# First block converted during attention, routing handed out by VectorE time, two groups' routing overlapped: attention and top-2 experts on one core

## Chip, core and metric

One core of a Trainium2 chip runs the whole program in one launch. The metric is device time in microseconds (us); smaller is better. Engines: PE (TensorE, matmul), PEld (its weight loads), DVE (VectorE), ACT (ScalarE), POOL (GpSimd) and SP (SyncE, which here only issues DMAs). Each engine takes its instructions in program order and waits on semaphores for the others.

## What is computed

```python
# attention: 8 batches x 8 heads, 576 positions in 9 chunks of 64, head size 64
scores = q_c @ k_c.T / sqrt(64);  attn = softmax(scores);  x = (attn @ v_c)   # -> x: 4608 tokens x 512
# experts: E = 8, hidden 1024
logits = x @ w_gate
noisy  = logits + log1p(exp(x @ w_noise)) * noise
top2   = argpartition(-noisy, 2)[:, :2];  top2_w = softmax over the two
for e in range(8):
    for k in range(2):
        mask = top2[:, k] == e
        h = maximum(x[mask] @ w1[e], 0)
        out[mask] += top2_w[mask, k] * (h @ w2[e])
```

## The kernel before

**Turns.** The 4608 tokens are 36 tiles of 128. The function `attend(it)` (L676) is one turn; it works on several tiles at different depths: `scores(it)` (L410, PE), the row maximum and subtraction (L418, L423, DVE) and the exponential (L428, ACT) of tile it; the transposes of the probabilities of tile it-1 (L430); the products with v (`pv`, L438) and the division (`norm_a/b/c`, L446 to L455) of tile it-2, which give the tile `xs`; and `x_trans` (L457) of tile it-3, which stores `xs` to a DRAM buffer `xbuf` by an SP DMA and transposes it for the gate. Once per four tiles come `gate_mm` (L468) and `gate_sum` (L476). Loads of q, k and v come in pairs of tiles, five buffers each (L363, L366); `xs` has three buffers.

**Routing.** The tiles form groups of 8, 8, 4, 8 and 8 (L160). `route(g)` (L487) is a Python generator, and its `yield`s only decide where its instructions stand in each engine's program order. Its steps: softplus of the noise logits on ACT (L500 to L503); noisy logits on DVE (L507 to L515); maxima and their indices (L520, L524); one-hots (L529 to L535); the *rank products* on PE (L541, L543), into PSUM bank 6; positions in the lists (L546 to L588, DVE); then for each tile r of the group a *list product*: `gohp` on POOL (L604) and ACT (L605, L606), `geq` on DVE (L608), `grhs` on POOL (L612; DVE for the last group), and two matmuls on PE (`place`, L596), two tiles behind. At the end the sums are added (L630), and `finish_lists` (L203) and `gather` (L233, POOL indirect DMAs) fetch the rows of a block of expert 0: block 0 after group 1, block 1 after group 3, block 2 after group 4.

**Who steps the routing.** `step_route(n)` (L651) advances the first generator of the list by n yields, each worth the same whatever it costs. A turn gives 2 yields between maximum and subtraction and 8 after the division (STEPS, L677; 3 and 12 from turn 33 on). To leave ACT and PE time, the routing has three stretches of 7 empty yields (IDLE, L485). A group's generator starts only when the one before it is done.

**Experts.** Each expert's list is cut into three blocks of 384 tokens or a little more. `x_tile(i, k)` (L277) is the *conversion* of 128 gathered rows of block i: for the first blocks, 4 PE transposes (L286) into PSUM bank 0 or 1, a rounded copy `xh` on ACT (L293) and the rest `xl` on DVE (L294). `layer1` (L305) is, for each of 8 hidden slices f, 4 steps d of 3 matmuls (`three`, L296, L303); its result leaves by `hh` (ACT, L321) and `hl` (DVE, L322); for block 0 it alternates between banks 0 and 1. `layer2` (L344) is 24 matmuls for each 128 tokens and starts in bank 6. While block 0 is in layer 1, the last four turns (`tail`, L733: what is left of tiles 33 to 35) and the splitting of the second weight matrix (`w_split`, L130, L138 on DVE) stand between its matmuls, and `hook_tail` (L737) gives 2 yields to the routing after each d step; `hook2_r` (L775) gives 2 after each f of layer 2, and layer 1 of block 1 gives 1 after each d.

After the 36 turns the kernel runs `attend(NT)`, then the three conversions of block 0 (L729, L730), then `layer1(0)`.

Of the kernel before, what the change touches and what calls it, by code (L numbers as in the profile page):

```python
# [60 lines left out]
def kernel(ctx, tc, qT, kT, vh, wgn, noise, w1, w2, out, caps=CAPS):  # L61
# [102 lines left out]
    xg = ctx.enter_context(tc.tile_pool(name="xg", bufs=5))  # L164

# [17 lines left out]
    XG, XH, HT, BX, BH, OB = {}, {}, {}, {}, {}, {}  # L183
    rot = {"xg": 0, "tr": 0, "l1": 0, "l2": 0}
# [92 lines left out]
    def x_tile(i, k):  # L277
# [5 lines left out]
        if i < NPE:  # L283
            src = bank("tr").rearrange("p (d n) -> p d n", d=ND)[:, :, 0:r]
# [103 lines left out]
    for j in range(3):  # L388
        load_q(j)
        load_k(j)  # L390
        load_v(j)
# [8 lines left out]
    load_q(3)  # L400
    load_k(3)
    load_v(3)
# [20 lines left out]
    def soft_sub(t, mx):  # L423
        PR[t] = work.tile([P, 512], FT, name="pr")
        nc.vector.tensor_tensor(by_head(PR[t]), sco(t), mx[:, :, :, None].to_broadcast([P, 2, 4, 64]), OP.subtract)
# [27 lines left out]
    def norm_c(t):  # L453
        XS[t] = work.tile([P, DM], FT, name="xs", bufs=3)
        nc.vector.tensor_tensor(by_head(XS[t]), pvb[:, :, :, 0:64], RC[t].to_broadcast([P, 2, 4, 64]), OP.mult)  # L455
# [29 lines left out]
    IDLE = 7  # L485

    def route(g):  # L487
# [16 lines left out]
        for _ in range(IDLE):  # L504
            yield

        V.scalar_tensor_tensor(u, u, -1.0, y, op0=OP.add, op1=OP.subtract)  # L507
        yield
        V.tensor_sub(sp, sp, u)
        yield  # L510
        V.scalar_tensor_tensor(sp, z[:, :, 1, :], 0.0, sp, op0=OP.max, op1=OP.add)
        yield
        V.tensor_mul(sp, sp, nz[:, t0:t0 + G, :])
        yield
        V.tensor_add(sp, sp, z[:, :, 0, :])  # L515
        yield
        m = gate.tile(n8, FT, name="gm")
        mi = gate.tile(n8, U32, name="gmi")
        for r in range(G):
            V.max(m[:, r], sp[:, r])  # L520
            if r % 2:
                yield
        for r in range(G):
            V.max_index(mi[:, r], m[:, r], sp[:, r])  # L524
            if r % 2:
                yield
        oh = gate.tile([P, 2, G, NE], FT, name="goh")
        for k in range(2):
            V.tensor_tensor(oh[:, k], be(e_row), br(mi[:, :, k]), OP.is_equal)  # L529
            yield  # L530
# [4 lines left out]
        V.tensor_sub(ex, m[:, :, 1], m[:, :, 0])  # L535
        yield
        nc.scalar.activation(ex, ex, AF.Exp)
        for _ in range(IDLE):
# [5 lines left out]
        for _ in range(IDLE):  # L544
            yield
# [4 lines left out]
        yield  # L550
# [3 lines left out]
        yield  # L554
# [3 lines left out]
        yield  # L558
        if g == LAST:
# [10 lines left out]
            yield  # L570
# [8 lines left out]
            yield  # L579
# [3 lines left out]
        yield  # L583
        pj = gate.tile([P, 2, 2, G], I32, name="gpj")
        pf = gate.tile([P, 2, 2, G], FT, name="gpf")
# [3 lines left out]
        yield  # L589

        lp = PS[:, 7, 0:2 * NL]
# [9 lines left out]
        for r in range(G):  # L601
# [8 lines left out]
            yield  # L610
# [3 lines left out]
            yield  # L614
            yield
            built.append((r, ohp, rhs))
            if len(built) > 2:
                yield
                place(*built.pop(0))
            yield  # L620
        while built:
            for _ in range(3):
                yield
            place(*built.pop(0))
        yield
# [6 lines left out]
        for i in EARLY:  # L632
            if g == EARLY[i]:
                js = slice(blocks[0][i][0][0], blocks[0][i][-1][0] + 1)
                finish_lists(lid0[i], lwt0[i], lfl[:, js, 0], a4[:, :, js, 0])
                gather(i)
        if g == LAST:
            for c in range(2):
                for js in (slice(0, NJ // 2), slice(NJ // 2, NJ)):
# [6 lines left out]
                    yield  # L646
# [15 lines left out]
    def finish_route(until=lambda: not routing):  # L662
        while not until():
            step_route(1)
# [11 lines left out]
    def attend(it):  # L676
        STEPS = 2 if it < 33 else 3  # L677
        if it % 2 == 0 and it >= 2 and it // 2 + 3 < NT // 2:
            load_q(it // 2 + 3)
            load_k(it // 2 + 3)  # L680
# [11 lines left out]
        if it - 5 >= 0 and (it - 5) % 4 == 3:  # L692
            gate_sum((it - 5) // 4)
            if grp_of[it - 5] != grp_of.get(it - 4):
                routing.append(route(grp_of[it - 5]))
        if it - 4 >= 0 and (it - 4) % 4 == 3:
            gate_mm((it - 4) // 4)
        if it < NT:
            mx = soft_max(it)
            step_route(STEPS)  # L700
            soft_sub(it, mx)
            soft_exp(it)
        if 0 <= it - 2 < NT:
            norm_b(it - 2)
            norm_c(it - 2)
            step_route(4 * STEPS)
        if it % 2 == 1 and it >= 3 and (it - 3) // 2 + 4 < NT // 2:
            load_v((it - 3) // 2 + 4)
# [12 lines left out]
    def block_bufs(q):  # L721
        pool = pb.enter_context(tc.tile_pool(name=f"blk{q}", bufs=1))
        HN = BN if q == 0 else 3 * P
        BX[q] = tuple(pool.tile([P, ND, BN], FR, name=f"x{c}{q}") for c in "hl")
# [4 lines left out]
    for k in range(len(blocks[0][0])):  # L729
        x_tile(0, k)  # L730

# [5 lines left out]
    def hook_tail(f, d):  # L737
# [6 lines left out]
        else:  # L744
            step_route(2)

    for i in range(NBL + 1):
# [27 lines left out]
        def hook2_r(k, f):  # L775
            hook2_f(k, f)
            step_route(2)
            if i == 0 and f == 6 and k < len(nxt):
                x_tile(1, k)
            if i == 1 and (k, f) in LATE:  # L780
# [8 lines left out]
        if i < NBL:  # L789
            layer1(i, hook1, hook_tail if i == 0 else lambda f, d: step_route(1))  # L790
# [160 lines left out]
```

## Time and profile before

| What | us |
|---|---|
| runs | 1015.87, 1020.08, 1020.49; median 1020.08 |
| the profiled execution: own time | 1020.72 |
| its span, first to last instruction | 1018.9 (1.8 lie around it) |
| PE busy in the span | 966.8 (95%) |
| first and last row maximum (36 turns) | 5.4 and 147.6 |
| last attention matmul group ahead of the first expert block | 152.69 |
| first layer-1 matmul | 158.73 |
| first layer-2 matmul | 187.10 |

A row of the timeline is: start, duration, engine, source line, operation, written tile and read tiles, count, and in brackets how long the engine had stood idle and what released it. A row of the waits is: the waiting engine and tile, what it waited for, total us, number of waits, longest one.

### The profile page before, as it was taken

To read this page: it belongs to the slowest core of one execution; us is meant where nothing else is said; L and a number is where in the kernel's file an instruction comes from. 1 tells how busy PE (TensorE), PEld (TensorE's weight loads), DVE (VectorE), ACT (ScalarE), POOL (GpSimd) and SP (SyncE) were. 2 spreads that over 40 slices of the span, in tenths; PEclk is the share of its full clock that TensorE was granted. 3 is DMA by queue.
4 is the path that set the end of the run, shared out by engine and by line. 5 is a ranking of instruction groups with operands and counts; after the bars stand their busy time and mean duration, and the time that the engine had idled before them with its cause. 6 is when DMAs were issued, how large, how long until landed. Compare 5 with 4: busy or idle time off the path is not lost.

```text
span 1018.9 us, 18401 instructions
## 1 busy us (share of the span) xinstructions
PE 966.8 (95%) x7353; PEld 862.0 (85%) x7353; DVE 458.5 (45%) x1001; ACT 310.4 (30%) x689; POOL 480.9 (47%) x619
## 2 busy tenths in 40 slices
PE   5888888999999999999999999999999999999994
PEld 4666767897889899989998999899989998899983
DVE  4676774644525353345334533453345334434311
ACT  3575855331314032213221322232223221323100
POOL 1033623324577668346834684477347825611111
PEclk9997988999999999999999999999999999999998
DMA  9999865233341543243423343344343334411212
GB/s 353 363 320 325 293 209 206 75 103 69 88 108 45 110 137 80 44 99 117 102 42 97 112 106 52 94 119 104 57 109 120 73 66 101 136 17 27 32 24 41
DMA packets 52233, 121.53 MB, mean 119 GB/s; under 512 B 8320, under 2 KB 9216, under 8 KB 52144
## 3 DMA queue, kind: packets, MB, share of 16 engines
q1 hardware_dynamic: 31984, 81.64, 22.2%
q0 software_dynamic: 20160, 38.69, 20.6%
q8 instruction: 58, 0.95, 0.4%
q14 instruction: 31, 0.25, 0.1%
HBM read 81.56 MB, written 38.73 MB: 118 GB/s over the span
## 4 chain that ended last, share of the span: by engine, by line
PE 82%; DVE 1%; ACT 1%; issue 0%; POOL 0%; ACTq 0%; DVEq 0%
PE PS L303 79%; PE PS L332 1%; PE PS L596 1%; PE PS L286 0%; DVE xl L294 0%; ACT xh L293 0%; DVE xs L455 0%; POOL gohp L604 0%; DVE o L341 0%; PE PS L220 0%; PE PS L443 0%; PE PS L470 0%; PE PS L482 0%; ACT gohp L605 0%; PE PS L222 0%
## 5 line engine op out<-in xcount | busy, mean ns | idle before, releaser
L258 POOL DMA_INDIRECT xg<-xbuf,piece x257 | 261.2, 1016 | 76.4 <-issue 68.4
L303 PE MATMUL PS<-xh,w1h 128*128 128x384 f32 (+2 forms) x768 | 263.0, 343 | 2.4 <-DVE xl L294 1.4
L303 PE MATMUL PS<-xl,w1h 128*128 128x384 f32 (+2 forms) x768 | 260.6, 339 | 0.3 <-DVE xl L294 0.3
L303 PE MATMUL PS<-xh,w1l 128*128 128x384 f32 (+2 forms) x768 | 260.6, 339 | 0.0
L303 PE MATMUL PS<-w2h,hh 128*128 128x512 f32 x584 | 229.4, 393 | 0.0
L303 PE MATMUL PS<-w2h,hl 128*128 128x512 f32 x584 | 228.2, 391 | 0.0
L303 PE MATMUL PS<-w2l,hh 128*128 128x512 f32 x584 | 228.1, 391 | 0.0
L270 POOL DMA_INDIRECT out<-o,lid x73 | 117.0, 1602 | 235.0 <-DVE o L341 213.5
L322 DVE SCALAR_TENSOR_TENSOR hl<-PS,hh 128x384 fp32r<-128x384 f32 (+1 forms) x192 | 107.1, 558 | 218.8 <-ACT hh L321 187.2
L321 ACT ACTIVATE hh<-PS 128x384 fp32r<-128x384 f32 (+1 forms) x192 | 94.1, 491 | 363.4 <-PE PS L303 314.3
L303 PEld LDWEIGHTS PS<-xh,w1h 128*128 128x128 f32 x768 | 144.4, 188 | 6.2 <-DVE xl L294 1.8
L303 PEld LDWEIGHTS PS<-xl,w1h 128*128 128x128 f32 x768 | 144.5, 188 | 2.3 <-DVE xl L294 0.5
L303 PEld LDWEIGHTS PS<-xh,w1l 128*128 128x128 f32 x768 | 144.4, 188 | 1.0
L341 DVE TENSOR_SCALAR o<-PS,lwt 128x512 f32<-128x512 f32 x73 | 54.5, 748 | 199.1 <-PE PS L303 166.6
L303 PEld LDWEIGHTS PS<-w2h,hl 128*128 128x128 f32 x584 | 109.6, 188 | 23.7
L303 PEld LDWEIGHTS PS<-w2h,hh 128*128 128x128 f32 x584 | 109.6, 188 | 23.3 <-issue 0.8
L303 PEld LDWEIGHTS PS<-w2l,hh 128*128 128x128 f32 x584 | 109.7, 188 | 22.5
L604 POOL TENSOR_SCALAR gohp<-row_p,gpf 128x128 f32<-128x128 f32 x36 | 26.3, 773 | 118.6 <-DVE gpf L588 107.0
L293 ACT ACTIVATE xh<-y 128x512 fp32r<-128x512 f32 x67 | 41.2, 615 | 106.7 <-DVE y L290 84.5
L294 DVE TENSOR_TENSOR xl<-y,xh 128x512 fp32r<-128x512 f32 x67 | 45.1, 673 | 48.3 <-ACT xh L293 31.8
L290 DVE STREAM_TRANSPOSE y<-xg 128x512 f32<-128x512 f32 x67 | 45.6, 680 | 2.4 <-DMA xg<-xbuf,piece 2.4
L138 DVE TENSOR_TENSOR w2l<-st,w2h 128x512 fp32r<-128x512 f32 x64 | 45.1, 705 | 0.0
(139 smaller groups left out, 798.9 us busy)
## 6 DMA issues: line engine op xcount, KB each, us to landing
st<-in_w SPq DMA_DIRECT2D x64, 512.0 KB
out<-zero SPq DMA_DIRECT2D x37, 256.0 KB
vb<-in_vh SPq DMA_DIRECT2D x18, 520.0 KB
xbuf<-xs SPq DMA_DIRECT2D x36, 256.0 KB
qp<-in_qT SPq DMA_DIRECT2D x17, 512.0 KB
kb<-in_kT SPq DMA_DIRECT2D x17, 512.0 KB
xg<-xbuf,piece POOLq DMA_INDIRECT x257
out<-o,lid POOLq DMA_INDIRECT x73
```

Source lines behind the costliest of these rows:

```text
L138: (eng or nc.vector).tensor_sub(lo[:, s], st[:, s], hi[:, s].bitcast(FT))
L258: nc.gpsimd.indirect_dma_start(out=XG[e, j][:, t * P:(t + 1) * P], out_offset=None, in_=xpieces, in_offset=bass.IndirectOffsetOnAxis(ap=pi ...
L270: s = nc.gpsimd.indirect_dma_start(out=to, out_offset=bass.IndirectOffsetOnAxis(ap=rows, axis=0), in_=o, in_offset=None, compute_op=OP.add)
L290: nc.vector.transpose(y[:, 0:4 * r], x[:, 0:4 * r])
L293: nc.scalar.activation(oh, src, AF.Copy)
L294: nc.vector.tensor_sub(ol, src, oh.bitcast(FT))
L303: nc.tensor.matmul(p, a, b, start=first and n == 0, stop=last and n == 2)
L321: nc.scalar.activation(hh[:, 0:m], p, AF.Relu)
L322: nc.vector.scalar_tensor_tensor(hl[:, 0:m], p, 0.0, hh[:, 0:m].bitcast(FT), op0=OP.max, op1=OP.subtract)
L332: nc.tensor.matmul(p[32 * q:32 * q + 32, 0:P], HF[0][:, f, 32 * t:32 * t + 32], w[:, q * P:(q + 1) * P], start=(f == 0), stop=(f == NF - 1))
L341: nc.vector.tensor_scalar(o[0:r], p[0:r], weights_of(i, j)[0:r], None, op0=OP.mult)
L604: nc.gpsimd.tensor_scalar(ohp[:, 0], row_p, pf[:, 0, 0, r:r + 1], None, op0=OP.is_equal)
```

## The change

1. **Conversions of block 0.** Its three conversions go into turns 33, 34 and 35, after the division of the turn; their transposes go to banks 6, 6 and 5 (bank 6 is otherwise the gate's and the rank products', bank 5 that of `x_trans`). Block 0's `xh`, `xl` get buffers of their own from the start (`bx0`). To make room, q, k, v have four pair buffers instead of five, `pr` two instead of three; `xs` gets five instead of three. The loads come one pair later in program order, the first ones in the order q0 k0 q1 k1 v0 q2 k2 v1, then v2.
2. **Steps by time.** Each yield carries an estimate of its DVE time in us, and `step_route(us)` runs steps until its budget is used up: 1.7 per turn (once, after the division and conversion), 0.8 per d step of layer 1 of block 0, 1.0 per second f of layer 2, 0.8 per second d of layer 1 of block 1. A bare `yield` ends the turn's work on that generator; it stands in place of the 7 empty ones.
3. **Overlap.** `routing` holds several generators. Once a group is at its list products (`placing`), a budget that is left over goes to the next group, which may run up to its own list products. The rank products aren't placed at the end of a turn with it % 4 == 2 nor of turns 32 and 33; block 2's gather waits in program order until block 1 is converted (`turned`).

```diff
-    vs = pa.enter_context(tc.tile_pool(name="vs", bufs=5, side="right"))
+    vs = pa.enter_context(tc.tile_pool(name="vs", bufs=4, side="right"))
...
-    loads = pk.enter_context(tc.tile_pool(name="loads", bufs=5))
+    loads = pk.enter_context(tc.tile_pool(name="loads", bufs=4))
...
-        XS[t] = work.tile([P, DM], FT, name="xs", bufs=3)
+        XS[t] = work.tile([P, DM], FT, name="xs", bufs=5)
...
         nc.scalar.activation(sp, u, AF.Ln)
-        for _ in range(IDLE):
-            yield
+        yield
 
         V.scalar_tensor_tensor(u, u, -1.0, y, op0=OP.add, op1=OP.subtract)
-        yield
+        yield 0.23
...
+        while turn[0] % 4 == 2 or turn[0] in (NT - 4, NT - 3):
             yield
...
+        placing.add(g)
+        while routing[0][0] != g:
+            yield
...
-            yield
+            yield 0.45
             rhs = gate.tile([P, 2, 2, NL], FT, name="grhs", bufs=3)
             B.tensor_tensor(rhs, eq[:, :, None, :].to_broadcast([P, 2, 2, NL]),
                             vals[:, :, t, :, None].to_broadcast([P, 2, 2, NL]), OP.mult)
-            yield
-            yield
+            yield 0.15
+            yield 0.15
             built.append((r, ohp, rhs))
             if len(built) > 2:
-                yield
+                yield 0.0
                 place(*built.pop(0))
-            yield
+            yield 0.0
...
-    def step_route(n):
-        for _ in range(n):
-            while routing:
+    def step_route(us):
+        for item in list(routing):
+            while us > 0:
                 try:
-                    next(routing[0])
+                    cost = next(item[1])
+                except StopIteration:
+                    routing.remove(item)
                     break
-                except StopIteration:
-                    routing.pop(0)
+                if cost is None:
+                    break
+                us -= cost
+            if us <= 0 or item in routing and item[0] not in placing:
+                return
...
             mx = soft_max(it)
-            step_route(STEPS)
             soft_sub(it, mx)
             soft_exp(it)
         if 0 <= it - 2 < NT:
             norm_b(it - 2)
             norm_c(it - 2)
-            step_route(4 * STEPS)
-        if it % 2 == 1 and it >= 3 and (it - 3) // 2 + 4 < NT // 2:
-            load_v((it - 3) // 2 + 4)
+            if 0 <= it - (NT - 3) < 3:
+                x_tile(0, it - (NT - 3), at=(6, 6, 5)[it - (NT - 3)])
+            step_route(1.7)
+        if it % 2 == 1 and it >= 3 and (it - 3) // 2 + 3 < NT // 2:
+            load_v((it - 3) // 2 + 3)
...
     attend(NT)
-    for k in range(len(blocks[0][0])):
-        x_tile(0, k)
-
...
             attend(tail.pop(0))
         else:
-            step_route(2)
+            step_route(0.8)
```

**Where the rows move.** Three places. First, PE at the end of attention; `xg` is the gathered block, `xs` the attention output, `pr` the probabilities, `ls` the gate, `xh` and `w1h` the operands of layer 1. Before, the last rows of turn 35, turn 36, then the conversions and layer 1:

```order
L463 MATMUL PS<-ident,xs 128x128 x4
L470 MATMUL PS<-xt,wg 32x512 x4
L443 MATMUL PS<-vb,pts 64x65 x16
L432 MATMUL PS<-ident,pr 128x128 x4
L463 MATMUL PS<-ident,xs 128x128 x4
L482 MATMUL PS<-sel,ls 128x16 x4
L286 MATMUL PS<-ident,xg 128x128 x12
L303 MATMUL PS<-xh_2715,w1h_1355 128x384
```

Now the end of turn 33, turn 34 and the beginning of turn 35 (a line of the changed file has a number two or three higher: L288 is L286 of before, L466 is L463), and after that the end of turn 36:

```order
L466 MATMUL PS<-ident,xs 128x128 x4
L288 MATMUL PS<-ident,xg 128x128 x4
L419 MATMUL PS<-kb,qp 64x64 x16
L446 MATMUL PS<-vb,pts 64x65 x16
L435 MATMUL PS<-ident,pr 128x128 x4
L466 MATMUL PS<-ident,xs 128x128 x4
L288 MATMUL PS<-ident,xg 128x128 x4
L419 MATMUL PS<-kb,qp 64x64 x16
```

```order
L446 MATMUL PS<-vb,pts 64x65 x16
L435 MATMUL PS<-ident,pr 128x128 x4
L466 MATMUL PS<-ident,xs 128x128 x4
L485 MATMUL PS<-sel,ls 128x16 x4
L305 MATMUL PS<-xh_136,w1h_1320 128x384
```

The 12 transposes of the conversions have moved from between turn 36 and layer 1 into the turns, four to a turn, and layer 1 follows directly on the last gate product.

Second, DVE in turns 12 and 13, where group 0's routing starts. Before:

```order
L455 TENSOR_TENSOR xs<-PS,rc 128x2x4x64
L507 SCALAR_TENSOR_TENSOR gu<-gu,gy 128x64
L509 TENSOR_TENSOR gsp<-gsp,gu 128x64
L511 SCALAR_TENSOR_TENSOR gsp<-gz_621,gsp 128x64
L420 TENSOR_REDUCE mx<-PS 128x8
```

Now (L458 is L455 of before, L423 is L420):

```order
L458 TENSOR_TENSOR xs<-PS,rc 128x2x4x64
L423 TENSOR_REDUCE mx<-PS 128x8
L428 TENSOR_TENSOR pr<-PS,mx 128x2x4x64
L454 RECIPROCAL rc<-rc 128x8
L458 TENSOR_TENSOR xs<-PS,rc 128x2x4x64
L507 SCALAR_TENSOR_TENSOR gu<-gu,gy 128x64
```

The first DVE step on ACT's softplus (`gu`) has moved back behind the maximum, subtraction and division of the next turn.

Third, PE in layer 1 of block 0, at group 3's list products (`grhs`, `gohp`). Before, where they lie closest:

```order
L596 MATMUL PS<-grhs,gohp 128x160 x2
L303 MATMUL PS<-xh_2715,w1h_1355 128x384
L303 MATMUL PS<-xl_2716,w1h_1355 128x384
L303 MATMUL PS<-xh_2715,w1l_1356 128x384
L303 MATMUL PS<-xh_2715,w1h_1587 128x384
L303 MATMUL PS<-xl_2716,w1h_1587 128x384
L303 MATMUL PS<-xh_2715,w1l_1588 128x384
L596 MATMUL PS<-grhs,gohp 128x160 x2
```

Now (L599 is L596 of before):

```order
L599 MATMUL PS<-grhs,gohp 128x160 x2
L305 MATMUL PS<-xh_136,w1h_1804 128x384
L305 MATMUL PS<-xl_137,w1h_1804 128x384
L305 MATMUL PS<-xh_136,w1l_1805 128x384
L599 MATMUL PS<-grhs,gohp 128x160 x4
L305 MATMUL PS<-xh_136,w1h_2035 128x384
L305 MATMUL PS<-xl_137,w1h_2035 128x384
L305 MATMUL PS<-xh_136,w1l_2036 128x384
L599 MATMUL PS<-grhs,gohp 128x160 x2
```

Between two tiles' list products stand 3 matmuls of layer 1 now, once none, where 6 to 9 stood. In all, layer 1 of block 0 holds the list products of 12 tiles now (group 2's four and group 3's eight; before it held group 3's eight) and the rank products of two groups (3 and 4), before those of group 3 alone. Group 4's list products have moved from layer 2 of block 0 and layer 1 of block 1 into layer 2 of block 0.

More of the change, by code (lines that the diff above doesn't have):

```diff
@@ L183 @@
     XG, XH, HT, BX, BH, OB = {}, {}, {}, {}, {}, {}
+    BX[0] = tuple(bx0.tile([P, ND, BN], FR, name=f"x{c}0") for c in "hl")
     rot = {"xg": 0, "tr": 0, "l1": 0, "l2": 0}
@@ L387 @@
     nc.scalar.preload_act_table_set("natural_log_exp_and_others")
-    for j in range(3):
+    for j in range(2):
         load_q(j)
         load_k(j)
-        load_v(j)
+    load_v(0)
+    load_q(2)
+    load_k(2)
+    load_v(1)
     wg = consts.tile([P, ND, 32], FT, name="wg")
@@ L423, in soft_sub @@
     def soft_sub(t, mx):
-        PR[t] = work.tile([P, 512], FT, name="pr")
+        PR[t] = work.tile([P, 512], FT, name="pr", bufs=2)
         nc.vector.tensor_tensor(by_head(PR[t]), sco(t), mx[:, :, :, None].to_broadcast([P, 2, 4, 64]), OP.subtract)
@@ L535, in route @@
         V.tensor_sub(ex, m[:, :, 1], m[:, :, 0])
+        yield 0.45
+        nc.scalar.activation(ex, ex, AF.Exp)
         yield
-        nc.scalar.activation(ex, ex, AF.Exp)
-        for _ in range(IDLE):
+        while turn[0] % 4 == 2 or turn[0] in (NT - 4, NT - 3):
             yield
@@ L582, in route @@
         V.tensor_mul(wt[:, 1], ex, wt[:, 0])
-        yield
-        pj = gate.tile([P, 2, 2, G], I32, name="gpj")
-        pf = gate.tile([P, 2, 2, G], FT, name="gpf")
+        yield 0.45
+        pj = gate.tile([P, 2, 2, G], I32, name="gpj", bufs=2)
+        pf = gate.tile([P, 2, 2, G], FT, name="gpf", bufs=2)
         V.tensor_scalar(pj[:, 0], lii[:, :, ts], NE * (P - 1), None, op0=OP.bitwise_and)
@@ L613, in route @@
                             vals[:, :, t, :, None].to_broadcast([P, 2, 2, NL]), OP.mult)
-            yield
-            yield
+            yield 0.15
+            yield 0.15
             built.append((r, ohp, rhs))
             if len(built) > 2:
-                yield
+                yield 0.0
                 place(*built.pop(0))
-            yield
+            yield 0.0
+        yield
         while built:
-            for _ in range(3):
-                yield
+            yield 0.4
             place(*built.pop(0))
-        yield
+        yield 0.0
         av = acc.rearrange("p c n -> p (c n)")
@@ L633, in route @@
             if g == EARLY[i]:
+                while i == 2 and not turned:
+                    yield
                 js = slice(blocks[0][i][0][0], blocks[0][i][-1][0] + 1)
@@ L676, in attend @@
     def attend(it):
[L677 to L680, printed above, removed]
+        turn[0] = it
+        if it % 2 == 0 and it >= 2 and it // 2 + 2 < NT // 2:
+            load_q(it // 2 + 2)
+            load_k(it // 2 + 2)
         if it in (12, 15, 18, 21):
@@ L723, in block_bufs @@
         HN = BN if q == 0 else 3 * P
-        BX[q] = tuple(pool.tile([P, ND, BN], FR, name=f"x{c}{q}") for c in "hl")
+        if q:
+            BX[q] = tuple(pool.tile([P, ND, BN], FR, name=f"x{c}{q}") for c in "hl")
         BH[q] = [tuple(pool.tile([P, HN], FR, name=f"h{c}{q}{f}") for c in "hl") for f in range(NF)]
```

51 lines of the change are left out of this document (29 added, 22 removed).

## The prediction

> **What bounds the kernel now.** I read the page first, then busy time by stretches, the waits, and the timeline where the stretches meet. The page:
>
> ```profile
> PE 966.8 (95%) x7353; PEld 862.0 (85%) x7353; DVE 458.5 (45%) x1001; ACT 310.4 (30%) x689; POOL 480.9 (47%) x619
> ```
>
> PE carries the span; a change that takes no matmul away can win only where PE stands still or runs on a slow clock. The execution's own time is 1020.72, 0.6 above the median of the runs; I sum against 1020.7. By stretches (columns: us; busy us and instructions of PE, PEld, DVE, ACT, POOL; granted clock; DMA share; GB/s):
>
> ```profile
> 5.40:47.10 41.70, 31.94 (x822) 25.93 (x822) 24.37 (x45) 20.49 (x44) 0.00 (x0) 0.96 1.01 380
> 47.10:151.70 104.60, 87.02 (x1922) 71.22 (x1913) 75.80 (x259) 70.11 (x179) 39.60 (x51) 0.90 0.84 292
> 240.00:1018.90 778.90, 764.38 (x4094) 690.90 (x4093) 307.33 (x509) 186.58 (x389) 406.68 (x515) 0.99 0.35 81
> ```
>
> The first two are the attention turns: PE is busy 77% and 83%, the clock is down to 0.90 on the mean in the second, DMA is full in the first. The last is dense matmul in an order that the change leaves alone. So the answer lies ahead of 240 us, in three stretches: A, the turns (to 153.5); B, from there to the first layer-2 matmul; C, the rest. The turns wait like this (DVE, 5 to 153 us):
>
> ```profile
> DVE mx L420 <- PE PS L416: 27.3, 20, 4.2
> DVE xs L455 <- DMA xbuf<-xs: 5.4, 2, 3.5
> DVE gr L552 <- ACT pr L428: 2.1, 1, 2.1
> ...
> DVE gu L507 <- ACT gsp L503: 1.9, 1, 1.9
> DVE gr L552 <- ACT gz L483: 1.0, 1, 1.0
> ```
>
> The 27.3 us on the scores are the dependence between engines within a turn; the change leaves it. The others are things that it touches. Between A and B, PE:
>
> ```profile
> 152.69 0.96 PE L482 MATMUL PS<-sel,ls 128*128 128x16 f32 x8
> 153.50 1.07 PE L286 MATMUL PS<-ident,xg 128*128 128x128 f32 x8
> 156.20 1.12 PE L286 MATMUL PS<-ident,xg 128*128 128x128 f32 x4 [1.63 <-DVE xl L294]
> 158.73 0.69 PE L303 MATMUL PS<-xh,w1h 128*128 128x384 f32 x1 [1.41 <-DVE xl L294]
> ...
> 159.94 0.46 PE L543 MATMUL PS<-gohb,ones 128*128 128x64 bf16 x8
> ...
> 167.98 0.45 PE L303 MATMUL PS<-xh,w1h 128*128 128x384 f32 x1 [0.99 <-DVE hl L322]
> ...
> 187.10 0.39 PE L303 MATMUL PS<-w2h,hh 128*128 128x512 f32 x1
> ```
>
> From 153.50 to 158.73 nothing but the conversions of block 0 happens on PE. B lasts 187.10 - 153.50 = 33.6 us.
>
> **The change, stretch A: the turns.** *Early turns, to 47.1.* `xs` waits 5.4 us for its store to leave its buffer; with five buffers it need not. But DMA ran at 380 GB/s there, at share 1.01, so the loads bind next. Four buffers for five mean one pair less fetched ahead:
>
> ```profile
> qp<-in_qT SPq DMA_DIRECT2D x17, 512.0 KB
> ```
>
> With k and v, which are as large, that is about 1.57 MB, or 4.1 us at 380 GB/s that DMA gets free. Between 0 and -5.4 I take **-3.5**.
>
> *Routing waits.* The steps on ACT's result (`gu`) and on the rank products (`gr`) now stand a turn behind what they wait for: 1.9 + 2.1 + 1.0. Next is PE, busy 83%, so the gain is between 0 and -5.0. I take **-5.0**: in these turns PE waits too.
>
> *Clock.* A mean of 0.90 over 104.6 us at levels of 1.00 and 0.50 is 20.9 us at half clock. The dips follow stretches where PE had little to do (the first two rows), and once one with small matmuls (the last two):
>
> ```profile
> 87.90:91.30 3.40, 0.76 (x33) 0.56 (x32) 2.92 (x11) 1.88 (x4) 0.43 (x1) 1.00 1.00 349
> 91.30:94.70 3.40, 3.16 (x40) 2.83 (x40) 3.31 (x27) 0.70 (x3) 1.27 (x1) 0.50 0.87 237
> ```
>
> ```profile
> 238.10:241.50 3.40, 2.25 (x19) 1.86 (x17) 1.02 (x2) 0.45 (x1) 0.00 (x0) 1.00 0.24 45
> 241.50:244.90 3.40, 3.40 (x11) 2.72 (x10) 1.06 (x3) 0.00 (x0) 1.11 (x2) 0.50 0.01 4
> ```
>
> Before, 10 yields of any cost delay the next scores; 1.7 us of budget and no steps ahead of the subtraction make such stretches rarer. Bounds: 0, and -10.5 if all 20.9 us ran at full clock on PE's path; I take **-3.0**, nearer to zero, since PE isn't alone on the path. PE's longest stand behind a subtraction was 2.2 us (and behind a load of k 4.3, at the very start):
>
> ```profile
> PE PS L416 <- DVE pr L425: 7.3, 5, 2.2
> PE PS L416 <- DMA kb<-in_kT: 6.2, 2, 4.3
> ```
>
> The Trainium skill (TensorE: Matmul & The Clock Gate, HAM oscillation) asks only for "no PE-idle gaps >~3.4µs". By that rule alone this term is nothing and the sum ends 3 us higher; the trace speaks against it, for none of the turns' stands behind a subtraction was that long.
>
> *Work that moves.* Out of A go group 2's rank products and four list tiles and the logits of group 3; into A come three conversions (each 0.69 on DVE and much the same on ACT, and PE's transposes) in turns that now hold no other steps:
>
> ```profile
> 157.98 0.69 DVE L294 TENSOR_TENSOR xl<-PS,xh 128x512 fp32r<-128x512 f32 x1 [1.24 <-ACT xh L293]
> ```
>
> Out: between 0 and -2.7 on PE, the rank products reckoned as a fifth tile (0.54 a tile, below); in: between 0 and 3 x 1.4 = 4.2, DVE and ACT in a row. I take -2.0 and +2.0, which cancel. The gather that feeds them is issued in turn 31 and first used in turn 33, some 7 us later. No row shows how long a gather takes to land; I take less than that, at no cost, and the other end is in the second rival.
>
> A: -3.5 - 5.0 - 3.0 = **-11.5**, or 142.0 for 153.5. For the 24 turns from 47.1 that is (104.6 - 8.0) / 24 = 4.0 us a turn, for 4.36.
>
> **Stretch B.** *Away:* 158.73 - 153.50 = 5.2; the `hl` wait, 1.0; and half of 4.3 us at clock 0.50 (158.7 to 163.0), 2.1. Left: 33.6 - 8.3 = 25.3.
>
> ```profile
> 156.20:163.00 6.80, 5.39 (x53) 4.12 (x54) 1.23 (x2) 0.86 (x2) 0.00 (x0) 0.50 0.00 0
> ```
>
> *Added PE work:* four list tiles and one group's rank products. From the chain of waits, a tile is 0.54, nine matmuls of layer 1 are 1.56, so three are 0.52:
>
> ```profile
> 177.25 0.54 PE PS L596 x4
> 177.79 1.56 PE PS L303 x9
> ```
>
> The rank products were 0.46 at half clock; I take 0.4 with their first one. 4 x 0.54 + 0.4 = 2.6; makes 27.9.
>
> *Added waits.* PE now meets a list tile every 0.54 + 0.52 = 1.06 us, and sometimes every 0.54. POOL makes its operands, one after the other (165 to 182 us, then 66 to 146 us):
>
> ```profile
> L604 POOL TENSOR_SCALAR gohp<-row_p,gpf 128x128 f32<-128x128 f32 x8 | 7.2, 900 | 23.1 <-DVE gpf L588 19.7 <-PE PS L596 3.5
> L612 POOL TENSOR_TENSOR grhs<-geq,vals 128x320 f32<-128x320 f32 x8 | 5.8, 722 | 0.0
> ```
>
> ```profile
> L604 POOL TENSOR_SCALAR gohp<-row_p,gpf 128x128 f32<-128x128 f32 x20 | 12.6, 630 | 88.8 <-DVE gpf L588 87.3 <-PE PS L596 1.4
> ```
>
> That is 0.900 + 0.722 = 1.62 us a tile beside layer 1, 0.63 + 0.72 = 1.35 in the turns. I take 1.5. What covered POOL before was the wider spacing, 6 matmuls and a tile, 1.58; that cover is gone. 12 tiles x (1.5 - 1.06) = 5.3, and 1.0 for the first tile and the place with two at once: 6.3. By 1.35 it is 4.5, by 1.62 7.7. One `gohp` there took far longer than the mean in the turns:
>
> ```profile
> 168.47 1.19 POOL L604 TENSOR_SCALAR gohp<-row_p,gpf 128x128 f32<-128x128 f32 x1
> ```
>
> The Trainium skill (SBUF — State Buffer, Who interferes with whom) has one of a DVE instruction with two SBUF inputs and a reading GpSimd instruction block the other for all its length. By that each tile's `geq` stops POOL as well as `w2l` does, the 1.62 holds, and B ends 1.4 us later; the mean that rises from 0.63 to 0.90 beside layer 1 agrees, though it doesn't show which instruction blocked which.
>
> *Group 4's rank products* stand on PE 15 matmuls (2.6 us) behind group 3's last tile; DVE must by then add the sums, finish the lists and do group 4's logits. Before, the same steps ran without a pause from 184.69 to 191.69, with two pairs of `hl` and `w2l` among them, one pair more than now (a pair is 0.56 + 0.85):
>
> ```profile
> 184.69 0.32 DVE L630 TENSOR_TENSOR acc<-acc,PS 128x160 f32<-128x160 f32 x1 [0.92 <-PE PS L596]
> ...
> 191.52 0.17 DVE L535 TENSOR_TENSOR gex<-gm 128x8 f32<-128x8 f32 x1
> ```
>
> ```profile
> L138 DVE TENSOR_TENSOR w2l<-st,w2h 128x512 fp32r<-128x512 f32 x5 | 4.2, 847 | 0.0
> L322 DVE SCALAR_TENSOR_TENSOR hl<-PS,hh 128x384 fp32r<-128x384 f32 x5 | 2.8, 558 | 6.3 <-ACT hh L321 6.2
> ```
>
> 7.0 less 1.4 are 5.6, against 2.6: a new wait of 3.0 on PE (0 if DVE has caught up, 4.4 with the pair). Behind it on PE are the rest of layer 1 and all of layer 2; on DVE nothing waits for it.
>
> B: 27.9 + 6.3 + 3.0 = 37.2, **+3.6**.
>
> **Stretch C.** One group's rank products fewer, **-0.4**; group 4's list products, closer together now, have DVE and POOL to themselves but for the conversions, so I add no wait; bounds 0 and the 6.3 that closeness costs in B. The stand ahead of 241.5 and its dip lie in an order that stays.
>
> Sum: 1020.7 - 11.5 + 3.6 - 0.4 = **1012.4**.
>
> **Rivals.**
> - *The turns gain all they can.* The 5.4 and 5.0 go whole, the clock dips bring 6.6: A -17. For it: PE, DVE and ACT are each under 84% busy. Against: DMA, busy 0.84 x 104.6 = 88 us of the second row. 1020.7 - 17 + 3.6 - 0.4 = 1006.9.
> - *Layer 1 gives it back.* A tile costs 1.91 (1.19 + 0.72) throughout: 12 x 0.41 = 4.9 more; and PE, a third idle, drops to half clock for two windows, 3 more. B +11.5: 1020.3. For it the dip after 2.25 busy of 3.4; against it the mean of 0.90. It is also the case that the early conversions don't do what they are for: if the gather lands late, PE, ACT and DVE wait in order and the 5.2 us return.
> - *The loads set the pace* (slower). DMA was full in the first row of the stretches and at 0.84 in the second, SP issues in order, and a pair's loads stand behind stores that wait for their turns; one pair less ahead, each of 14 pairs comes 1 us late: 1012.4 + 14 = 1026.4. It makes the kernel slower by more than 0.5% from 0.9 us a pair on. Against it: only two waits for a load of k, at the start.
>
> **How the numbers follow.** Forecast 0.50, all gained 0.18, given back 0.21, loads 0.11. 0.5% is 5.1 us, about what a measurement of this kernel can tell from no change. Faster by more: the first two, 0.68; within: 0.21; slower: 0.11. The range runs from 1004 (the first rival, less 1.8 for tiles at 1.35 and 1 of the 3.0) to 1021 (the second), leaving out the third and the tails.
>
> **Right or wrong.** Right: last attention gate product near 142; no `xs` wait on a store; layer 1 directly behind; PE waits at L599 on POOL totalling 4 to 8 us between there and layer 2, and one of some 3 us at a rank product. Wrong: scores that wait for DMA in mid-attention, turns still 4.3 us apart, or dips to half clock inside layer 1.

## The result and the profile after

The changed kernel takes 1025.15 us, median of 11 runs (1021.85 to 1027.19), against 1019.02 for the kernel before (11 runs, 1014.97 to 1024.29): a ratio of 1.0062, 95% interval 1.0041 to 1.0082. It is 0.6% slower; the forecast was 1012.4 and faster. The profiled execution of the changed kernel took 1021.93, one of its shortest, with a span of 1020.1; the profiled execution of before took 1020.72.

The row of busy times on the page, after:

```profile
PE 968.0 (95%) x7353; PEld 861.1 (84%) x7353; DVE 459.6 (45%) x1001; ACT 310.7 (30%) x689; POOL 477.8 (47%) x619
```

The work is nearly the same (PE 968.0 us for 966.8). Busy time by stretches, after (columns: us; busy us of PE, PEld, DVE, ACT, POOL; granted clock; DMA share; GB/s): the turns 0 to 12, the turns 12 to 35, and layer 1 of block 0:

```profile
5.32:47.31 41.99, 32.94 (x822) 26.63 (x822) 24.62 (x44) 20.46 (x44) 0.00 (x0) 0.96 0.99 364
47.31:141.52 94.21, 80.58 (x1864) 67.71 (x1858) 72.02 (x227) 65.73 (x164) 34.43 (x43) 0.93 0.91 317
147.73:187.90 40.17, 32.40 (x220) 26.86 (x220) 25.14 (x130) 19.02 (x54) 20.86 (x27) 0.96 0.47 171
```

Layer 1 of block 0 before, in the same columns:

```profile
158.73:187.10 28.37, 27.38 (x194) 25.07 (x194) 14.77 (x41) 15.12 (x39) 13.52 (x17) 0.92 0.54 204
```

So layer 1 starts 11.0 us earlier (147.73 for 158.73) and takes 11.8 us longer (40.17 for 28.37); it ends 0.8 later than before. By PE's last matmul another 1.15 us are lost (1008.00 for 1006.05). Everything that was won ahead of layer 1 is lost inside it.

DVE's waits in the turns, after (engine, tile, what it waited for: total us, times, longest):

```profile
DVE mx L423 <- PE PS L419: 27.9, 19, 3.5
DVE rc L454 <- ACT rc L451: 5.6, 7, 1.9
DVE xl L296 <- ACT xh L295: 3.1, 3, 1.9
DVE acc L633 <- PE PS L599: 1.5, 1, 1.5
```

The waits of `xs` on its store and of `gu` and `gr`, 10.4 us before, are gone, as forecast. In their place stand waits on ACT (5.6 for the denominators, 2.0 before; 3.1 for the early conversions). PE's largest waits in turns 12 to 35, before and then after:

```profile
PE PS L416 <- DVE pr L425: 5.8, 4, 2.2
PE PS L443 <- issue: 2.6, 4, 1.6
```

```profile
PE PS L446 <- issue: 6.5, 5, 2.2
PE PS L419 <- DVE pr L428: 2.8, 4, 1.0
PE PS L419 <- issue: 2.1, 3, 1.2
```

"issue" means that PE waited for nothing that the profile shows. These waits have grown from 2.6 to 8.6 us, while PE's other waits in these turns fell from 13.8 to 4.7; they are taken up below. In layer 1 of block 0 PE waits, after:

```profile
PE PS L599 <- POOL grhs L615: 4.5, 5, 1.6
PE PS L542 <- DVE gohb L533: 2.4, 1, 2.4
PE PS L305 <- DVE hl L324: 0.7, 1, 0.7
```

The tiles' weight loads (PEld), which run beside PE's matmuls, wait for POOL more often: once at each of the 12 tiles. Before, they had no such wait in layer 1.

```profile
PEld PS L599 <- POOL grhs L615: 8.1, 12, 1.9
```

The timeline of PE there (start, duration, engine, line, tile, count, idle time ahead and its releaser) shows list tiles and layer-1 matmuls in turn:

```profile
151.31 0.81 PE L599 MATMUL PS<-grhs,gohp 128*128 128x160 f32 x4 [1.06 <-POOL grhs L615]
...
152.59 0.81 PE L599 MATMUL PS<-grhs,gohp 128*128 128x160 f32 x4
153.13 0.44 PE L305 MATMUL PS<-xh,w1h 128*128 128x384 f32 x1
153.41 0.34 PE L305 MATMUL PS<-xl,w1h 128*128 128x384 f32 x1
153.59 0.33 PE L305 MATMUL PS<-xh,w1l 128*128 128x384 f32 x1
154.09 0.81 PE L599 MATMUL PS<-grhs,gohp 128*128 128x160 f32 x4 [0.17 <-POOL grhs L615]
...
167.48 0.81 PE L599 MATMUL PS<-grhs,gohp 128*128 128x160 f32 x4 [1.58 <-POOL grhs L615]
...
170.68 0.81 PE L599 MATMUL PS<-grhs,gohp 128*128 128x160 f32 x4 [1.12 <-POOL grhs L615]
...
178.03 0.81 PE L599 MATMUL PS<-grhs,gohp 128*128 128x160 f32 x4
...
184.77 0.22 PE L542 MATMUL PS<-gohb,before 128*128 128x72 bf16 x1 [2.35 <-DVE gohb L533]
```

Group 3's eight tiles go from 167.48 to 178.03, (178.03 - 167.48) / 7 = 1.51 us each, where PE's own work would allow 1.06. POOL needed 0.79 for `gohp` and 0.73 for `grhs` there, 1.52 a tile. From the wait ahead of 184.77 on, the clock is at half for 3.4 us:

```profile
184.20:187.60 3.40, 2.83 (x17) 2.83 (x17) 2.58 (x14) 1.10 (x3) 0.04 (x1) 0.50 0.39 128
```

### The profile page after: what moved, and what is told of

It is laid out like the page before. It is cut to its first block, busy times and chain, and to the rows that moved or that the text cites. A ratio compares the mean times of both kernels' runs of the same rounds, so it can differ in the third digit from the quotient of the medians.

```text
span 1020.1 us, 18447 instructions
## 1 busy us (share of the span) xinstructions
PE 968.0 (95%) x7353; PEld 861.1 (84%) x7353; DVE 459.6 (45%) x1001; ACT 310.7 (30%) x689; POOL 477.8 (47%) x619
## 4 chain that ended last, share of the span: by engine, by line
PE 81%; DVE 2%; POOL 1%; issue 1%; ACT 1%; POOLq 0%; ACTq 0%
PE PS L305 78%; PE PS L334 1%; PE PS L599 1%; POOL grhs L615 0%; POOL gohp L607 0%; PE PS L288 0%; DVE w2l L138 0%; PE PS L466 0%; DVE xl L296 0%; PE PS L473 0%; DVE gaccp L650 0%; ACT xh L295 0%; DVE grhs L648 0%; PE PS L485 0%; DVE hl L324 0%
## 5 line engine op out<-in xcount | busy, mean ns | idle before, releaser
L419 PEld LDWEIGHTS PS<-kb,qp 64*64 64x64 f32 x1152 | 23.9, 152 | 25.1 <-DVE pr L428 8.7
```

The costliest lines, as they stand in the source:

```text
L419: nc.tensor.matmul(PS[s, h, o:o + 64], q[r, t % 2, hp, s], k[r, t % 2, hp, s], start=True, stop=True)
```

## Experiments

Sixteen runs. Times are ratios to the kernel before on the same chip; layer 1, turns and waits are from each run's one profile. The time of turns 0 to 35 runs from the first row maximum to the start of the last one.

**The parts apart.** Two kernels took the change in halves. The early conversions with the change's buffers, routing as before:

```diff
-            step_route(4 * STEPS)
+            if 0 <= it - (NT - 3) < 3:
+                x_tile(0, it - (NT - 3), at=5)
+            step_route(4 * STEPS)
```

> The kernel before with the change's buffers and early conversions of block 0 (their transposes all go to bank 5), the routing still stepped as before. Theory C (the early conversions pay, and what the change loses is lost by the routing's new places): 158.73 - 153.50 = 5.2 us of conversions alone go, less 1 to 2 us in the turns, so the first layer-1 matmul at 154 to 155.5 us for 158.73, and 3 to 5 us off the time. Rival N (the turns pay for the conversions what layer 1 saves): the first layer-1 matmul at 157 to 160 us, the time within 0.2%.

Measured: 0.9978 (0.9953 to 1.0003). Layer 1 started at 151.77 but took 29.81 us, with a new wait:

```profile
PE PS L544 <- DVE gohb L536: 2.4, 1, 2.4
```

The place of layer 1 speaks for theory C; the time, 2.2 us less with an interval that reaches no change, falls between the two theories. The routing by time alone, conversions behind turn 36:

```diff
-            if 0 <= it - (NT - 3) < 3:
-                x_tile(0, it - (NT - 3), at=(6, 6, 5)[it - (NT - 3)])
...
     attend(NT)
+    for k in range(len(blocks[0][0])):
+        x_tile(0, k)
```

> The changed kernel without its early conversions and with the buffers of before (five pairs, xs three, pr three); the routing handed out by time and overlapped as in the change. Theory C: the first layer-1 matmul at 151 to 154 us, layer 1 of block 0 lasts about 40 us as in the changed kernel (40.2, before 28.4), and the time is 3 to 6 us longer than the changed kernel's (ratio to before 1.009 to 1.012). Rival N: the same time as the changed kernel (ratio 1.004 to 1.008).

Measured: 1.0094 (1.0059 to 1.0128), layer 1 started at 149.51 and took 39.89 us. The loss belongs to the routing; the two halves, -0.2% and +0.9%, add up to the change's +0.6% within 0.1. Turns 0 to 35 took 132.5 us here, less than in any profile with the early conversions (135.2 or more); against the changed kernel's 136.2 most of the difference lies in the last three turns, 8.9 us for 11.2.

**The early turns.**

```diff
-        XS[t] = work.tile([P, DM], FT, name="xs", bufs=3)
+        XS[t] = work.tile([P, DM], FT, name="xs", bufs=5)
```

> The kernel before with five buffers for xs instead of three, nothing else. Theory L (the loads set the pace of the early turns, whatever the buffers): the 5.4 us wait of xs on its store goes, scores wait for loads instead, the row maximum of turn 12 stays at 46.5 to 47.5 us (47.07 before) and the time within 0.3%. Rival D (the fewer buffers for q, k and v of the change took back what the xs buffers gave): with the five pair buffers kept, turn 12 comes at 42 to 44 us and the time falls by 3 to 5 us.

Measured: 1.0008 (0.9984 to 1.0031), turn 12 at 47.20. Its waits and its busy time in turns 0 to 12:

```profile
DVE mx L420 <- PE PS L416: 16.8, 10, 2.5
```

```profile
5.54:47.20 41.66, 31.67 (x822) 25.72 (x822) 24.54 (x44) 20.43 (x44) 0.00 (x0) 0.96 1.02 394
```

The store's 5.4 us are gone, the wait on scores has grown from 12.8 to 16.8, and the stretch lasts 41.66 us as before (41.62), with DMA full. With four pair buffers and the new order of loads:

```diff
-    loads = pk.enter_context(tc.tile_pool(name="loads", bufs=5))
+    loads = pk.enter_context(tc.tile_pool(name="loads", bufs=4))
```

> The kernel before with four pair buffers of q, k and v instead of five and the change's order of loads, nothing else. Theory L: turn 12 at 46.5 to 48 us, the time within 0.2%. Rival D: turn 12 at 49 us or later, the time 3 to 6 us longer.

Measured: 1.0005 (0.998 to 1.003). Turn 12 came at 49.85, in rival D's range, but turn 24 at 99.26, no later than before (99.79), and the time is the same. Theory L holds for the time: neither buffers nor depth buy anything here. In all eighteen profiles these twelve turns last 40.8 to 44.1 us.

**The changed kernel once more.**

> The changed kernel once more, unaltered, beside the three that follow, for a second profiled execution. Theory S (the loss sits in layer 1 of block 0 and is the same in every execution; the turns differ from one execution to the next): layer 1 of block 0 lasts 39.5 to 41 us again (40.17), the turns 12 to 35 lie anywhere from 91 to 98 us (94.2), ratio to before 1.004 to 1.009. Rival V (layer 1 varies as well, and its 40.2 us were one execution's): layer 1 off by more than 2 us.

Measured: 1.0066 (1.0041 to 1.009), layer 1 40.13 us, turns 0 to 35 138.5 (136.2 in the first). The waits in layer 1 are the same to 0.05 us. What happens in layer 1 repeats; the turns do not.

**What layer 1 waits for.** First POOL's load:

```diff
-        B = nc.gpsimd if g < LAST else V
+        B = nc.gpsimd if g < 2 else V
```

> The changed kernel with grhs of groups 2 and 3 made on DVE (0.50 us each, as group 4's) instead of POOL. Theory P (POOL's 1.5 us a tile sets the pace of the 12 list tiles of layer 1): the waits of PE at list tiles, 4.7 us, fall under 1.5; layer 1 of block 0 at 32 to 35.5 us for 40.2; the time 5 to 7 us under the changed kernel's. Rival Q (the tiles are too close for any engine; DVE, given 12 x 0.5 = 6 us more, is late with hl and with group 4's gohb instead): layer 1 at 37 to 41 us, with PE waiting 4 us or more for DVE.

Measured: 1.004 (1.002 to 1.0059); layer 1 37.38 us. Theory P falls: moving `grhs` gains 2.8 us, not 5 to 8. Layer 1 lies in rival Q's range, but by another wait than Q named: `hl` (0.7) and `gohb` (2.4) wait as before, and four tiles now wait for DVE's `grhs`:

```profile
PE PS L599 <- DVE grhs L615: 3.3, 4, 1.3
```

Nor are the tiles too close for any engine. Where the operands are there, a tile every 3 matmuls costs no wait and stands at PE's own pace, 1.07 us (two tiles, with the three matmuls between them left out):

```profile
171.81 0.70 PE L599 MATMUL PS<-grhs,gohp 128*128 128x160 f32 x4
...
172.88 0.71 PE L599 MATMUL PS<-grhs,gohp 128*128 128x160 f32 x4
```

Then the rank products:

```diff
+        for _ in range(6 if g == LAST else 0):
+            yield
-        rk = PS[:, 6, 128:128 + 8 * (G + 1)].rearrange("p (g e) -> p g e", e=NE)
+        rk = PS[:, 2 if g == LAST else 6, 128:128 + 8 * (G + 1)].rearrange("p (g e) -> p g e", e=NE)
```

> The changed kernel with group 4's rank products six steps later (behind the start of layer 2 of block 0) and in PSUM bank 2, which is free there. Theory R (the 2.35 us wait at the rank products is a term of its own, with the half clock of 3.4 us behind it worth 1.5): layer 1 of block 0 at 36 to 38 us for 40.2, the time 2 to 4 us under the changed kernel's. Rival G (POOL's waits grow into the room, or the steps of group 4 come late in layer 2 and the wait returns there): layer 1 plus layer 2 of block 0 within 1 us of 62.8, the time within 0.1% of the changed kernel's.

Measured: 1.0044 (1.0023 to 1.0064); layer 1 36.09 us, 4.1 less: the wait, the half clock and the products themselves went. To the second block's layer 2 it is 77.98 for 81.05 us, so 3.1 of it stays won. Theory R holds for layer 1; the time fell by 0.2% against the unaltered kernel beside it, with intervals that overlap. Both together:

> Both edits together: grhs of groups 2 and 3 on DVE, and group 4's rank products six steps later in bank 2. Theory P and R: the terms add, layer 1 of block 0 at 29.5 to 33 us, the time 7 to 10 us under the changed kernel's and 1 to 4 us under before. Rival Q: no better than the better one of the two alone.

Measured: 1.0023 (1.0000 to 1.0046), layer 1 33.08, 7.1 less: the two terms add (2.8 + 4.1 = 6.9). It is still not under before, short of what was expected.

**How close the tiles stand.** The changed kernel with 2.3 us a turn, so that group 2's tiles lie in the turns again, and one tile in 6 matmuls of layer 1:

```diff
-            step_route(1.7)
+            step_route(2.3)
...
-        else:
+        elif d % 2:
             step_route(0.8)
```

with group 4's rank products in bank 2.

> The changed kernel with a budget of 2.3 us a turn instead of 1.7 (so group 2's list tiles lie in the turns again and 8 tiles instead of 12 in layer 1 of block 0), steps only after every second d step of layer 1 of block 0 (a tile every 6 matmuls instead of 3), and group 4's rank products, which then come in layer 2, in bank 2. Theory D (the tiles' closeness, not their number alone, cost the 11.8 us): layer 1 of block 0 at 28 to 30.5 us, from its start to layer 2 of block 1 69 to 72 us (81.0 in the changed kernel, 69.2 before), the turns 0 to 35 as in the changed kernel's executions (135 to 139 us), and the time 8 to 11 us under the changed kernel's, ratio to before 0.993 to 0.998. Rival T (the turns pay in full for the tiles and steps that they take back): turns 0 to 35 at 140 us or more, ratio to before 0.999 or more.

Measured: 1.003 (1.0006 to 1.0055). Layer 1:

```profile
155.07:180.91 25.84, 25.45 (x195) 23.77 (x195) 17.02 (x67) 15.23 (x42) 11.80 (x17) 1.00 0.62 234
```

25.84 us with 0.4 of waits: better than theory D asked. But turns 0 to 35 took 142.5 us, as rival T said, though one profile of the turns says little (see the five below). The same without the spacing:

> As the run beside it (2.3 us a turn, group 4's rank products in bank 2), but with steps after every d step of layer 1, as in the changed kernel: a tile every 3 matmuls, 14 of them in layer 1 of block 0. The sum of tiles outside the turns is the same 16. Theory D: from the start of layer 1 of block 0 to layer 2 of block 1 77 to 80 us, 6 to 9 us more than the spaced run, ratio to before 1.000 to 1.004. Rival M (only the number of tiles outside the turns matters): within 2 us of the spaced run.

Measured: 1.0152 (1.0109 to 1.0195). Layer 1 and its waits:

```profile
157.88:201.42 43.54, 33.36 (x236) 29.72 (x236) 30.63 (x137) 20.89 (x59) 20.41 (x28) 0.96 0.47 168
```

```profile
PE PS L542 <- DVE gohb L533: 5.6, 2, 3.5
PE PS L599 <- POOL grhs L615: 2.9, 2, 2.5
PE PS L599 <- DVE grhs L615: 1.7, 3, 0.8
```

To the second block's layer 2 it takes 79.67 us, the spaced run 68.70, with the same 16 tiles outside the turns (all 16 in layer 1 here, where 14 were expected): 11.0 us, more than theory D's 6 to 9. These are the price of handing out the steps twice as fast, and the waits say what it consists of: 5.6 us at two sets of rank products and 4.6 at five places with list tiles, each time for operands that DVE or POOL had not finished. The other tiles passed without a wait.

**What the routing costs the turns.** The kernel before with both `step_route` calls of a turn taken out and groups 0 to 3 routed in one row behind turn 36:

```diff
-            step_route(STEPS)
...
-            step_route(4 * STEPS)
...
     attend(NT)
+    finish_route()
```

> The kernel before with no routing steps in the turns at all: groups 0 to 3 (28 list tiles, four sets of rank products) are routed in one row behind turn 36, ahead of the conversions of block 0; the order is the kernel's own otherwise. What this asks is what the routing costs the turns. Theory F (most of it lies beside other work or is paid in the turns only in part, so taking steps out or handing them out better has little to win): turns 0 to 35, 138 to 142 us in executions of the order before, last 131 to 137 us, so that 20 tiles with all their steps cost 5 to 9 us there. Rival H (the turns pay for the routing in full, and a better hand-out could win the 8 us that were forecast): 120 to 128 us.

Measured: 1.0503 (1.0467 to 1.0539), as the row makes it 78.6 us from the last row maximum to layer 1. The turns from 12 on:

```profile
47.05:131.65 84.60, 68.32 (x1748) 55.39 (x1745) 50.56 (x92) 51.50 (x114) 10.15 (x8) 0.94 0.94 337
```

Turns 0 to 35 took 126.0 us: rival H's range. Theory F falls. The order before took 142.2, 140.7 and 138.2 in three profiles (before, five `xs` buffers, four pair buffers), 140.4 on the mean. So 20 tiles with all their steps cost the turns some 14.4 us, 0.72 a tile, by one execution of the bare turns. That execution ran on another chip, where before has a median of 1009.53 us, 7.5 less than on the chip of the first runs (1017.01). Some 4.4 of this lie in the blocks behind (773.1 us from layer 2 of the second block to the last matmul, 777.5 on the mean of the three profiles); the other 3 may be in the turns, so 14.4 is an upper value. Less 3 it would still be more than theory F's 5 to 9.

**The fastest version.** Early conversions, routing as before, and the 2.4 us wait at group 3's rank products answered by eight more yields ahead of them (group 4's in bank 2):

```diff
         nc.scalar.activation(ex, ex, AF.Exp)
-        for _ in range(IDLE):
+        for _ in range(IDLE + (8 if g == 3 else 0)):
             yield
```

> The kernel before with the early conversions (as the run with these alone), and group 3's rank products eight yields (four d steps, 2.1 us) later in layer 1, since PE waited 2.40 us for them there; group 4's in bank 2. Theory R: the wait goes, layer 1 of block 0 at 27.3 to 28.2 us for 29.8, ratio to before 0.993 to 0.997. Rival L (group 3's lists are then late for the gather of block 1, and PE waits for its first conversion in layer 2): from the start of layer 1 to layer 2 of block 1 still 70.6 us, ratio 0.997 to 0.999.

Measured: 0.9991 (0.9964 to 1.0019), layer 1 26.11 us. The wait went, the median hardly. Side by side with the early conversions alone on another chip:

> The early conversions alone once more, as the yardstick for the run beside it on the same chip. Theory A (what leaves layer 1 leaves the whole time): ratio to before 0.996 to 0.999, layer 1 of block 0 29.8 us with its 2.4 us wait. Rival B (the turns' scatter decides): the two runs of this call within 0.1% of each other.

> Early conversions and group 3's rank products four d steps later, once more. Theory A: 2 to 4 us (0.2 to 0.4%) under the run beside it, ratio to before 0.992 to 0.996, layer 1 of block 0 26 to 27.5 us. Rival B: within 0.1% of the run beside it, though layer 1 is as short.

Measured: 1.0003 (0.9982 to 1.0024) and 0.995 (0.993 to 0.9971), medians 1017.24 and 1013.59. Layer 1 29.78 and 26.12 us; PE's only wait left there:

```profile
PE PS L446 <- DVE xs L458: 0.8, 1, 0.8
```

Theory A holds: what leaves layer 1 (3.7 us) leaves the time (3.65). By its ratios this version is faster than the changed kernel both times, and faster than before in this pair; its two ratios put that gain at 0.1 to 0.5%.

**PE's own instructions.** The "issue" waits of the turns. A stand in the timeline of the changed kernel:

```profile
108.12 0.41 PE L446 MATMUL PS<-vb,pts 64*64 64x65 f32 x16
110.74 0.46 PE L446 MATMUL PS<-vb,pts 64*64 64x65 f32 x16 [2.21 <-issue]
```

It cuts a row of 32 like matmuls in the middle. To ask whether full DMA is the cause, the 16 zero writes of turns 20 to 35 were moved into layer 1:

```diff
-        if 20 <= it < NT:
-            zero_out(1)
```

> The changed kernel without the 16 zero writes to out in turns 20 to 35 (256 KB each, 4.2 MB); all of them come in layer 1 of block 0, where the others are. Theory I (PE's instruction blocks come late because data fills DMA in the turns): PE's stands at the 16 KB places in turns 12 to 35 fall from 4.4 to 9.4 us to under 3, these turns last 86 to 91 us (92 to 101 in the executions so far), and the time falls by 3 to 6 us. Rival J (the stands do not hang on the share of DMA that data takes): 4 us or more of them again, turns 12 to 35 at 92 us or more, the time within 0.2% of the changed kernel's.

Measured: 1.0043 (1.0022 to 1.0065). Turns 24 to 35 in the changed kernel and in this one, then the stands of this one in turns 12 to 35:

```profile
95.00:141.52 46.52, 40.09 (x916) 34.47 (x912) 34.01 (x101) 32.11 (x80) 18.55 (x23) 0.92 0.87 299
```

```profile
95.00:141.60 46.60, 39.27 (x922) 33.86 (x913) 35.09 (x112) 32.65 (x80) 18.68 (x23) 0.93 0.73 247
```

```profile
PE PS L419 <- issue: 4.9, 4, 1.8
PE PS L446 <- issue: 2.6, 2, 2.2
...
PE PS L473 <- issue: 0.6, 1, 0.6
```

The DMA share fell from 0.87 to 0.73; PE stood as long as before (8.1 us for 8.6), and turns 12 to 35 took 94.1 us for 94.2. Rival J holds. The same edit to the fastest version:

> Early conversions, later rank products and the old steps, with the same 16 zero writes moved into layer 1. Theory I: little, since PE stands only 0.6 to 1.0 us at such places here: ratio to before 0.990 to 0.995 (0.995 without the edit). Rival J: the same ratio within 0.1%, or longer if the zeros then hold up the first store of block 0.

Measured: 0.9979 (0.9959 to 0.9998); in layer 2 of block 0 PE then waits 0.84 us for a gathered row. No gain over the version without the edit, whose two ratios were 0.9991 and 0.995.

## Why the prediction was wrong

The profiled executions differ by +1.2 us where -8.3 was forecast: 9.5 us to account for. Three steps of the sum failed: the gain in the early turns (-3.5), which the loads did not allow; the gain in the later turns (-8.0), of which -1.6 is left on the mean; and in B the waits and the half clock of layer 1, 3.0 us more than summed.

| Step | forecast | measured |
|---|---|---|
| early turns, to turn 12 | -3.5 | +0.2 |
| turns 12 to 35 (routing waits, clock, moved work) | -8.0 | -6.3 |
| last turn's end | 0 | +0.3 |
| B: end of attention to layer 2 (33.6 before) | 37.2 | 40.2 |
| C | -0.4 | +1.15, and 0.7 less behind the last matmul |

1. **"Between 0 and -5.4 I take -3.5"** failed outright. The text itself said that the loads bind next, and then credited the shallower fetch with 4.1 us of DMA. The loads do bind: with five buffers alone the wait moves from `xs` to the scores (12.8 to 16.8) and the stretch stays at 41.66 us. The right value was the bound 0.

2. **"-5.0" for routing waits and "-3.0" for the clock** look nearly right in this pair of profiles, but that is the luck of the pair. The same order of turns lasts 136.2, 138.5, 137.0, 142.9 and 135.2 us in five profiles of the changed order (the run itself, the repeat, and the three runs that alter layer 1 alone), 138.0 on the mean, against 140.4 before: -2.4, less than the 7.7 us by which these five differ among themselves. The profile of before that the sum rested on was the slowest of its three. On the means, turns 12 to 32 last 84.5 us for 85.3: neither the hand-out by time nor the four tiles fewer gained anything clear of the scatter there. The last three turns show less scatter, and there "-2.0 and +2.0, which cancel" can be told apart: 12.6 us before, 8.9 with the routing by time alone, so taking routing steps out is worth 3.7 (one profile); 11.9 in the changed order, so the conversions cost 3.0 there (in the old order 1.1, 13.8 for 12.6). With 20 tiles in the turns again, steps by time gave 142.5 and 145.7, no better than the old yields.

   The clock moves between executions too. From turn 12 to 35 the mean granted clock was 0.90, 0.90 and 0.98 in the three profiles of the old order and 0.92 to 0.96 in the five of the changed one, so the 20.9 us at half clock that the term started from were those of one execution. The waits on `gu` and `gr` did go; PE's stands for its own instructions came: 2.6 us before, 8.6 in the changed kernel. This is the wait that took their place, and no rival had it.

3. **B's new work and new waits were right in kind**: "PE waits at L599 on POOL totalling 4 to 8 us" (4.5), "one of some 3 us at a rank product" (2.4), and the 1.5 us a tile (1.51). "Left: 25.3" was right (the spaced run, with 8 tiles, has 25.45 outside its waits), and so was the 2.6 of added PE work (four tiles at 0.55 and the rank products are 2.5). PE's busy time rose by more, 32.4 less 25.45 are 6.95, but only because the rows hide part of the waiting: 1.7 of it is half of 3.4 us at half clock, and the rest, some 3, are tiles that stand later than PE's own pace without a wait of PE's being named. From 151.31 to 152.59, for instance, it is 1.28 us, not 1.06; the weight load of that tile waits 0.27 for POOL's `grhs`. Measured from the matmul ahead of a tile to the one behind it (0.61 us before, and 1.15 for two tiles in a row), the 12 tiles take 7.6 us longer in all, the 4.5 among them. What failed is the sizes and one term left out: the half clock behind the new wait (1.7), which the forecast had only removed, not added; the wait on POOL, 7.6 for 6.3; and the `hl` wait that was to go (1.0) and stayed at 0.7. The rank wait was 0.6 shorter than summed. Together that is some 3, and B took 40.2 for 37.2.

4. **"The conversions go, 5.2"** was right: from the last turn's row maximum to layer 1 it was 11.11 and is 6.21. But alone they gained 0.2% in one pair and nothing in the other, since the time they take in the turns (1.1 us in the last three) and a 2.4 us wait at the rank products, which before did not have, come off it.

The rival **"layer 1 gives it back"** named 1020.3 and came nearest. Its mechanism was only partly the one at work: a tile cost 1.51, not 1.91, and one window of half clock came, not two. The shallower loads ("the loads set the pace") did nothing to the time: ruled out by the run with four buffers. Of the signs listed, the dip to half clock inside layer 1 was there and so was layer 1 directly behind the turns; the last gate product came at 146.91, not near 142.

What the medians say fits: -2.4 in the turns, -4.9 behind them, +11.8 in layer 1 make +4.5, against a measured 0.62% or 6.3 us (4.2 to 8.4). C's +1.15 is no finding: from layer 2 of the second block to PE's last matmul the five profiles of the changed order lie between 774.9 and 780.9 us (before 778.1).

## What to carry to other kernels

Work that is taken out of a stretch in which several engines wait for each other is paid again where it lands: price it there at the pace of its slowest maker, and keep a spacing that gives this maker its time (with one list tile in 6 matmuls PE did not wait; steps handed out twice as fast cost 11 us, nearly all of it where operands were not ready). A row of PE can look busy and still be late: look at the waits of its weight loads as well. When a wait is removed, look which resource is already full beside it before crediting anything. Before summing against one profile, see how far the same stretch moves between executions: here 8 us in the turns and 6 in the blocks at the end, but 0.05 in layer 1 (two profiles).

## What was not expected of the hardware

PE seems to stand for its own instructions. Counted over the trace, the longer "issue" stands of the turns lie 127 matmuls apart, or a multiple of it to within one (at matmul 347, 474, 727, 854, 1742, 1869, 1996 and 2122 in the changed kernel, 220, 347, 727 and 854 before). With a weight load each these are 254 instructions. At each of them a packet of 16,384 bytes on an instruction queue has just come in: it takes some 1.0 us, and PE goes on some time after its start (108.44 to 109.40 us, PE on at 110.74). This time is much the same everywhere: over all eighteen profiles it is 2.2 to 2.6 us at 137 of the 145 stands of over 0.25 us at such places up to turn 35. The stands were up to 3.2 us long. That the packet is what PE stood for is read from these times; no run moved the packets themselves.

The Trainium skill (Runtime: NRT & Kernel Launch, Instruction fetch mechanics) has instructions refilled in 16 KiB blocks of 256 and calls the cost of crossing such a boundary "mostly hidden". The block size agrees with the 127 matmuls and 16,384 bytes; the rest does not hold in these turns, where 8.1 to 13.3 us of PE's time from turn 12 to 35 went into "issue" stands, most of it at such places, in six profiles of the changed order (8.6, 9.3, 9.5, 13.3, 9.6, and 8.1 without the zero writes).

The stands are no mark of the changed order, though. They are long where PE waits little for anything else from turn 12 to 35:

| Turns 12 to 35 | other waits of PE, us | "issue" stands, us |
|---|---|---|
| bare turns | 3.0 | 12.7 |
| changed order, six profiles | 4.7 to 6.3 | 8.1 to 13.3 |
| routing by time alone | 5.1 | 8.3 |
| steps as before, seven profiles | 12.7 to 14.3 | 1.9 to 4.4 |
| steps as before, without the zero writes | 14.0 | 6.1 |
| 2.3 us a turn, two profiles | 19.9 and 20.2 | 1.8 and 0.7 |

So a wait that is taken out of these turns seems to come back in part as a stand, because PE reaches the place before the packet does; no run shows that by itself. Why the packet starts so late is open: a DMA share of 0.73 for 0.87 did not change it.
